# Three loads in place of two for the first block of x, and five pieces in place of six for w2, in a fused attention and gated-FFN kernel

## Chip, cores and metric

One core of one Trainium2 chip. The experiments ran on five different chips, each next to the kernel before in the same rounds. The metric is the device time of one execution in microseconds (us). The span of a trace is 1.8 us shorter than the time of the same execution: 1936.4 against 1938.2 in the profiled run of the kernel before. A "look" below is one profiled run; a load "lands" when the profile shows all of it arrived.

## The reference, cut to what matters

```python
x = A_x                                   # 1 x 2048 x 640, bf16
xn = layernorm(x)
# attention, 32 heads of 192, 2048 keys:
q = (xn @ wq) per head;  p = softmax(q k^T * 192**-0.5);  s = (p v) @ wo
# gated FFN on the same xn:
g = silu((silu(xn @ w1) * (xn @ w3)) @ w2)
return x + s * g
```

## The kernel before

The stream of work is 32 heads x 4 blocks of 512 queries, and TensorE (PE) is busy in it almost without a gap. What matters here is the head of the kernel, in which block 0 of x is loaded, normalised and transposed before PE has anything useful to do.

```python
def load_x(g, t0=0, t1=4, queue=nc.sync):        # row tiles t0..t1 of block g
    queue.dma_start(out=x_sb[:, 4 * g + t0:4 * g + t1, :],
                    in_=x2[g * 512:(g + 1) * 512, :].rearrange("(p t) d -> p t d", t=4)[:, t0:t1, :])

def swap_halves(g):                              # SBUF to SBUF, behind the transposes
    qs = slice(g * 512, (g + 1) * 512)
    nc.sync.dma_start(out=xnS[0:64, :, qs], in_=xnT[64:P, :, qs])
    nc.sync.dma_start(out=xnS[64:P, :, qs], in_=xnT[0:64, :, qs])

def head_start():
    load_x(0, 0, 2)                # SP queue
    load_x(0, 2, 4)                # SP queue
    load_k0(0, nc.sync)            # half of K of head 0
    load_w0()                      # weights of head 0, three loads on the GpSimd queue
    turn_over(44)                  # 44 matmuls without a use, to keep PE going
    ln_stats(0, 0)                 # VectorE, row tile 0
    ln_stats(0, 1)                 # VectorE, row tile 1
    ln_stats_act(0, 3)             # ScalarE, row tile 3: two passes with sums
    load_k0(1, nc.scalar)          # these three loads stand behind tile 3 on ScalarE
    load_x(1, queue=nc.scalar)
    load_v(0, (0,), nc.scalar)
    ln_stats(0, 2)                 # VectorE, row tile 2
    ...                            # rstd of tiles 2 and 3: needs ScalarE's sum
    for i in range(4):
        ln_norm(0, i, nc.vector)
    ln_turn(0, 0, nc.scalar.copy)  # PE: the first transposes ("pst")
    turn_k0(pk0, 0, range(4))      # PE: transposes of K ("pk")
    ...
    swap_halves(0)
    ...
    project_first()                # q of head 0, then the first scores ("st")

# in the stream, at head 16:
for c0, c1 in _pieces(FC, -(-FC // 6)):          # six pieces of two chunks
    nc.sync.dma_start(out=wrest["w2"][:, c0:c1, :], in_=B_w2...[:, c0:c1, :])
```

`x2...rearrange("(p t) d")` gives each partition four consecutive rows. A load of two tiles has 128 contiguous pieces of 2,560 bytes, a load of one tile 128 of 1,280 bytes.

## Time and profile before

| | before |
|---|---|
| time, median of 3 runs | 1938.26 us (1937.99 to 1938.29) |
| PE busy | 1926.6 of 1936.4 us |
| tile 0's statistics start on VectorE | 3.58 us |
| ScalarE's first pass over tile 3 starts | 4.66 us |
| PE's first transposes start | 7.60 us |
| first score matmul | 13.10 us |
| first matmul that reads the swapped half xnS | 19.05 us |

The page's lines, the chain of waits in the head and the pause at 19.05 us are shown in the prediction. Lines of the timeline: columns are start, length, engine, line, operation, output<-input, count, and in brackets the idle time ahead with what ended it.

```profile
2.77 3.89 PE L572 MATMUL pk<-ident_bf 128*128 128x128 bf16 x44 [2.77 <-POOL ident_bf masks.py:199]
...
8.25 1.06 PE L271 MATMUL pk<-ident_bf,kn 128*128 128x128 bf16 x16
```

The 44 filler matmuls end at 6.66 and the first transposes start at 7.60, so PE pauses 0.94 us. The 16 transposes of K take 1.06 us.

### The profile page before, as it was taken

What the parts mean: (1) busy time and instruction counts of PE and PEld (TensorE: products, weight loads), DVE (VectorE), ACT (ScalarE), POOL (GpSimd) and SP (SyncE); (2) the same over time, 40 slices, a digit from 0 to 9 for tenths busy, and PEclk for the clock granted to TensorE, in tenths of its full rate; (3) what the DMA queues carried; (4) which work ended last, traced back from release to release, by engine and by line L of the source; (5) the groups of instructions that cost most, each with busy time, mean ns of one, the idle gap of its engine ahead of it and who ended that gap; (6) DMA issues with size and microseconds to landing.
All of it is one profiled execution on the core that took longest, in us unless ns stands there. A gap on an engine that the chain in (4) does not pass through costs nothing.

```text
span 1936.4 us, 59669 instructions
## 1 busy us (share of the span) xinstructions
PE 1926.6 (99%) x27273; PEld 1315.6 (68%) x27281; DVE 654.6 (34%) x997; ACT 1180.0 (61%) x1279; POOL 282.5 (15%) x501
## 2 busy tenths in 40 slices
PE   9999999999999999999999999999999999999998
PEld 6666666666666666666666666666666666577776
DVE  7333333333333333333333333333333334521111
ACT  6677676767676767776777777677767677210000
POOL 3111111111111111111111111111111110000000
PEclk9999999999999999999999999999999999999999
DMA  8643433323333434363434343434334220937783
GB/s 181 129 101 67 98 68 86 84 62 88 59 90 61 100 63 97 68 162 69 101 66 100 69 101 69 101 64 101 69 69 96 58 68 2 260 69 137 151 152 62
DMA packets 394643, 178.98 MB, mean 92 GB/s; under 512 B 341616, under 2 KB 382832, under 8 KB 394384
## 3 DMA queue, kind: packets, MB, share of 16 engines
q1 hardware_dynamic: 371136, 125.32, 31.6%
q0 software_dynamic: 19472, 45.71, 10.0%
q8 instruction: 215, 3.52, 0.8%
q10 hardware_dynamic: 3776, 4.06, 0.7%
q14 instruction: 44, 0.36, 0.1%
HBM read 52.82 MB, written 27.79 MB: 42 GB/s over the span
## 4 chain that ended last, share of the span: by engine, by line
PE 99%; DVE 1%; DMA 0%; ACT 0%; issue 0%; DVEq 0%; ACTq 0%
PE obank L519 35%; PE st L487 34%; PE ps L424 14%; PE ps_s L111 11%; PE ps_f L731 3%; PE ps_gu L705 1%; PE st L488 1%; PE ps L410 0%; DVE stats L316 0%; DMA x_all<-in_A_x_dram 0%; PE ps L391 0%; PE pst L354 0%; PE pk L271 0%; DVE xn L346 0%; ACT pT L493 0%
## 5 line engine op out<-in xcount | busy, mean ns | idle before, releaser
L493 ACT ACTIVATE pT<-st 128x1024 bf16<-128x1024 f32 (+1 forms) x1025 | 1046.1, 1021 | 250.2 <-PE st L488 234.0
L519 PEld LDWEIGHTS <-pT 64*128 64x128 bf16 x16384 | 711.3, 94 | 242.3 <-ACT pT L493 0.6
L519 PE MATMUL obank<-vt,pT 64*128 64x193 bf16 x16384 | 849.7, 243 | 0.0
L487 PE MATMUL st<-qC,KW 64*128 64x512 bf16 x2046 | 605.6, 376 | 0.1
L528 DVE COPY osum<-obank 128x772 f32<-128x772 f32 x128 | 123.1, 962 | 787.1 <-PE obank L519 787.1
L488 PE MATMUL st<-qB,KW 64*128 64x512 bf16 x1024 | 385.0, 376 | 0.0
L487 PE MATMUL st<-qA,KW 64*128 64x512 bf16 x1022 | 384.3, 376 | 0.1
L488 PE MATMUL st<-qC,KW 64*128 64x512 bf16 x1022 | 384.3, 376 | 0.0
L488 PE MATMUL st<-qA,KW 64*128 64x512 bf16 x1022 | 384.3, 376 | 0.0
L487 PEld LDWEIGHTS <-KW 64*128 64x128 bf16 x3068 | 278.5, 94 | 153.7 <-issue 2.1
L424 PE MATMUL ps<-xnT,W 64*128 64x512 bf16 x1280 | 297.2, 376 | 0.0
L424 PE MATMUL ps<-xnS,W 64*128 64x512 bf16 x1280 | 296.0, 376 | 0.0
L488 PEld LDWEIGHTS <-KW 64*128 64x128 bf16 x3068 | 278.5, 94 | 0.5
L377 POOL DMA_DIRECT2D qC<-qA x124 | 65.4, 528 | 1283.0 <-DVE rl_all L535 1268.2
L430 ACT CAST qB<-ps 128x512 bf16<-128x512 f32 x131 | 76.7, 585 | 228.2 <-PE ps L424 222.6
L111 PE MATMUL ps_s<-wo_sb,oT 128*128 128x384 bf16 (+3 forms) x1535 | 208.8, 299 | 0.1
L424 PEld LDWEIGHTS <-W 64*128 64x128 bf16 x2560 | 122.9, 94 | 121.4 <-issue 0.2
L111 PEld LDWEIGHTS <-oT 128*128 128x128 bf16 x1536 | 148.4, 98 | 60.4
L529 DVE TENSOR_TENSOR osum<-osum,obank 128x772 f32<-128x772 f32 x128 | 122.7, 959 | 13.4
L536 DVE TENSOR_TENSOR ostage<-osum,rl_all 128x768 bf16<-128x768 f32 x128 | 122.7, 958 | 6.3 <-DMA o_scr<-ostage 1.9
L465 DVE SCALAR_TENSOR_TENSOR hT<-pt,qB 64x512 bf16<-64x512 bf16 x64 | 43.8, 684 | 197.4 <-ACT pt L464 197.4
L429 DVE CAST qA<-ps 128x512 bf16<-128x512 f32 x131 | 90.6, 692 | 25.3 <-PE ps L410 7.2
(84 smaller groups left out, 621.9 us busy)
## 6 DMA issues: line engine op xcount, KB each, us to landing
o_scr<-ostage SPq DMA_DIRECT2D x16, 1536.0 KB, 10.6
vt<-in_A_v_cache_dram SPq DMA_DIRECT2D x63, 384.0 KB, 5.9
qC<-qA POOLq DMA_DIRECT2D x248, 64.0 KB, 1.9
qC<-qB POOLq DMA_DIRECT2D x124, 64.0 KB, 2.3
wo_sb<-in_A_wo_dram POOLq DMA_DIRECT2D x1, 7680.0 KB, 36.1
W<-in_A_wq_dram POOLq DMA_DIRECT2D x32, 160.0 KB, 3.6
W<-in_B_w_dram POOLq DMA_DIRECT2D x32, 80.0 KB, 3.3
W<-in_A_wq_dram POOLq DMA_DIRECT2D x32, 80.0 KB, 3.0
```

Source lines behind the costliest of these rows:

```text
L111: nc.tensor.matmul(ps[:, 0:w], lhsT=oT[:, k, :], rhs=wo_sb[:, k, c0:c1], start=(k == 0), stop=(k == OC - 1))
L377: nc.gpsimd.dma_start(out=qC[0:64, half, :], in_=qAB[half][64:P, :])
L424: nc.tensor.matmul(ps[:, r * 512:(r + 1) * 512], lhsT=W[rows, j, :], rhs=xs[rows, j // 2, qs], start=(j == 0), stop=(j == 2 * DC - 1))
L429: a = nc.vector.tensor_copy(out=qAB[0][:], in_=ps[:, 0:512])
L430: b = nc.scalar.copy(out=qAB[1][:], in_=ps[:, 512:1024])
L487: nc.tensor.matmul(st2[:, 0:512], lhsT=ka, rhs=qa, start=r == 0 and nr == 3, stop=r == nr - 1)
L488: nc.tensor.matmul(st2[:, 512:1024], lhsT=kb, rhs=qb2, start=r == 0 and nr == 3, stop=r == nr - 1)
L493: nc.scalar.activation(out=pT2[:, c * w:(c + 1) * w], in_=st2[:, c * w:(c + 1) * w], func=ACT.Exp, scale=att_scale)
L519: nc.tensor.matmul(obanks[r][:, j * 256:j * 256 + DH + 1], lhsT=pT2[r * 64:(r + 1) * 64, t * 512 + j * P:t * 512 + (j + 1) * P], rhs=vt[r ...
L528: nc.vector.tensor_copy(out=osum[:], in_=ov[0])
L529: nc.vector.tensor_tensor(out=osum[:], in0=osum[:], in1=ov[1], op=ALU.add)
L536: nc.vector.tensor_tensor(out=ostage[:, qb * 4:qb * 4 + 4, hg * DH:(hg + 1) * DH], in0=osum[:, :, 0:DH], in1=rl.unsqueeze(2).to_broadcast( ...
```

## The change

Its intent: tile 0's statistics can start when 160 KB have landed and not 320, so the chain that begins the kernel gets shorter; and w2 costs the SP queue one issue less.

```diff
-            for c0, c1 in _pieces(FC, -(-FC // 6)):
+            w2_cuts = [FC * i // 5 for i in range(6)]
+            for c0, c1 in zip(w2_cuts, w2_cuts[1:]):
                 nc.sync.dma_start(out=wrest["w2"][:, c0:c1, :], in_=B_w2.rearrange("(c p) d -> p c d", p=P)[:, c0:c1, :])
@@
     def head_start():
 
-        load_x(0, 0, 2)
+        load_x(0, 0, 1)
+        load_x(0, 1, 2)
         load_x(0, 2, 4)
         load_k0(0, nc.sync)
```

## The prediction

> **What bounds the kernel now.** I read the page first (busy shares, the chain that ended last), then that chain in order of time, then busy time by stretch, then the waits around the head, and last the DMA queues in steps of half a microsecond or one.
>
> The page says that TensorE is the bound, and the busy time by stretch says where it is not:
>
> ```profile
> span 1936.4 us, 59669 instructions
> PE 1926.6 (99%) x27273; PEld 1315.6 (68%) x27281; DVE 654.6 (34%) x997; ACT 1180.0 (61%) x1279; POOL 282.5 (15%) x501
> ...
> 0.00:12.50 12.50, 8.79 (x112) 8.32 (x113) 7.10 (x22) 6.39 (x9) 7.23 (x14) 1.00 0.84 245
> ...
> 50.00:831.00 781.00, 780.95 (x12061) 532.07 (x12058) 265.97 (x372) 551.83 (x585) 131.27 (x234) 1.00 0.39 82
> 831.00:882.00 51.00, 51.00 (x794) 34.77 (x790) 17.35 (x24) 36.74 (x41) 8.42 (x15) 1.00 0.57 154
> ```
>
> In a stretch line come its length, then the busy time of PE, PEld, DVE, ACT, POOL, the clock, the DMA share and GB/s. All idle time of PE together is 1936.4 - 1926.6 = 9.8 us. Of it 3.7 us lie in the first 12.5 us, and from 50 to 831 us there is 0.05 us. Most of the rest (5.8 us) lies after 1722 us, in the output, which the change does not touch. So only the head can give anything, and the last stretch shown, in which w2 is loaded, has nothing to give.
>
> The chain in the head, start and length in us:
>
> ```profile
> 0.75 2.81 DMA x_all<-in_A_x_dram
> 3.56 0.02 issue
> 3.58 0.90 DVE stats L316 x2
> ...
> 7.13 0.06 DVE ve L590
> 7.19 0.36 DVE xn L346
> 7.55 0.05 issue
> 7.60 0.81 PE pst L354 x10
> 8.41 0.89 PE pk L271 x16
> ...
> 10.31 2.20 PE ps L391 x20
> ```
>
> The first load of x (two row tiles, 320 KB) lands at 3.56; from there VectorE runs without a pause (statistics of rows 0, 1, 2, then the normalisation at 7.19), and PE's first useful work starts at 7.60. So the chain does begin with the load that the change cuts. But there is a second gate further on. The timeline at 19 us, and below it the DMA issues from 12.1 to 12.4 us (count, KB each, us to landing):
>
> ```profile
> 18.76 0.10 PEld L424 LDWEIGHTS <-W 64*128 64x128 bf16 x2
> 18.84 0.38 PE L424 MATMUL ps<-xnT,W 64*128 64x512 bf16 x1
> 19.05 0.39 PE L424 MATMUL ps<-xnS,W 64*128 64x512 bf16 x2
> 19.05 1.82 PEld L424 LDWEIGHTS <-W 64*128 64x128 bf16 x18 [0.19 <-issue]
> ...
> xnS<-xnT SPq DMA_DIRECT2D x1, 320.0 KB, 7.4
> ```
>
> Everywhere later (46.39, for one) the xnT and the xnS matmul of a pair start together, and the chain gives the 20 matmuls 2.16 us; here the xnS one starts 0.21 us late and the 20 take 2.36 us in the chain. The last line is the copy of one half of the normalised x to the other 64 partitions (the half swap, two transfers), issued on SP at 11.57 and landing 7.4 us later, at 18.97: just before 19.05. The profile calls the pause "issue", but I read it as a wait for that transfer. So PE already waits some 0.2 us for a DMA at 19.05, and whatever is won before it counts only if that DMA lands earlier too.
>
> Does it? The queues by stretch (q1 is SP's, q10 ACT's, q0 GpSimd's), for 9 to 10, 12 to 13 and 14 to 15 us:
>
> ```profile
> q10 hardware_dynamic: 184, 0.35, 99.9%
> ...
> q0 software_dynamic: 82, 0.14, 92.6%
> ...
> q1 hardware_dynamic: 192, 0.19, 106.3%
> ```
>
> Each line is packets, MB, share of the 16 engines. From about 6.6 to 11.4 us the engines serve what ACT issued at 5.53 to 6.44 (half of K, x of block 1, half of V); then to about 13 the weights of head 1, which GpSimd had issued from 8.05 on; only then the half swap, issued at 10.81. It is a backlog, worked off at a share of about 1.
>
> **What the Trainium skill says.** "Perfetto Trace Analysis", DMA Optimizations: splitting a DMA lets some pieces start sooner, and it adds the condition that the DMA engines are generally idle. Before 2 us the trace agrees; from 2.5 us on the share is 0.87 to 1, so the condition doesn't hold behind the first tile. "DMA: Bandwidth & Descriptors", Issuing engines are not separate DMA queues: transfers of all issuers run on the same 16 engines, and the issuing engine only saves issue time. The trace agrees: one queue's transfers wait while another's are served. The same page, Why small descriptors are slow, gives each packet a fixed overhead; the trace has it too, larger, as worked out below.
>
> **The change part by part.**
>
> *First tile of x alone.* 160 KB instead of 320 KB. SP's queue moved 0.12 MB from 1.5 to 2.5 us and 0.38 MB in the next microsecond; 0.328 MB are reached at about 3.05, 0.164 MB at about 2.62. The landing came 0.5 us after the first of these, so tile 0 lands at about 3.1 instead of 3.56: -0.45 us for the first statistics.
>
> *Second tile alone.* It lands at about 3.6. VectorE needs it 1.07 us after it began tile 0, at 4.2: hidden.
>
> *Tiles 2 and 3 one issue later.* An issue on SP takes 0.44 us (0.88 for two). Issued at 1.63 instead of 1.19, with a first byte 1.0 us after issue (0.75 to about 1.75 in the trace), the third load can run from 2.65, before the first two are through at 3.05. So the issue itself is hidden. But the cut rows give 256 packets of 1,280 B for 128 of 2,560 B. From 8 to 9 us packets of about 4,240 B took 0.944 x 16 / 92 = 164 ns; from 2.5 to 3.5 us those of about 2,330 B took 16 / 163 = 98 ns; the line through both has 17 ns per packet. 8 more per engine: +0.14 us. So tiles 2 and 3 land at about 4.75 instead of 4.62.
>
> *Chain to PE.* VectorE runs 0.45 us earlier up to the step at L590, which needs ScalarE's sum over tile 3 (ready at 6.45, now about 6.6). It would get there at 7.05 - 0.45 = 6.6: a tie. PE's first transposes then start at about 7.2 instead of 7.6, and its K transposes, which need K landed (1.68 + 6.0 = 7.68), at about 7.8 to 7.9. So PE is some 0.3 to 0.4 us ahead at 13 us.
>
> *At 19.05.* The half swap is issued 0.3 to 0.4 us earlier, but into the same backlog. That backlog starts with ACT's issues, which follow ScalarE's first pass over tile 3 (landing 4.62, pass from 4.66, issue 5.53), and before it, from 6 to 7 us, the DMA engines are partly idle (121 and 189 GB/s). So the whole queue hangs on tile 3, which is not earlier but about 0.14 us later. I therefore choose: the swap lands at 18.97 + 0.0 to 0.15, PE waits 0.6 us there instead of 0.2, and the 0.3 to 0.4 us are given back.
>
> *w2 in five pieces.* Chunks 2, 2, 3, 2, 3 instead of six times 2: one issue of about 0.5 us fewer on SP at 840 us, the same bytes. The loads land by about 858 us, the first reader of that tile starts at 1644, and PE is 51.00 us busy in the 51 us around them. 0.0 us.
>
> *Sum.* Head -0.35, given back at 19.05 +0.35, later landing of tile 3 +0.1, w2 0.0: +0.1 us, 1938.36. I pull that to 1938.2 for the second rival below.
>
> **Rivals.**
> 1. The head's gain goes through to the end: the swap is issued 0.4 us earlier and lands 0.4 us earlier. For it: its packets alone are on the engines from 13 us on, so a latency of the SBUF-to-SBUF copy and not the backlog might set its landing. Against it: first packets appear 1.5 us or more after the issue, exactly when the queues before it end. Time 1937.85.
> 2. Part of it goes through: the swap's packets get in among the weights of head 1. Time about 1938.05.
> 3. ScalarE's tile 3 and with it every transfer behind comes the whole issue time later (0.44 us), if the loads are not pipelined as I assume. The chain from tile 3 then delays the swap by as much. Against it: the loads were served without a gap before. Time 1938.7.
> 4. A result over 2% needs 39 us, four times PE's whole idle time to gain, or a new wait repeated in all 128 blocks to lose; nothing in the change touches a block after the first but w2's loads.
>
> **Range and chances.** The mechanism gives 1937.85 (everything goes through) to 1938.7 (whole issue time lost); the three runs of before spread by 0.3 us. I give half to "given back", a third to rivals 1 and 2, the rest to rival 3: 1938.2, range 1937.7 to 1938.6. Within 2% is all but certain: 0.98, 0.01 each side for what I can't see.
>
> **What would show it.** Tile 0's statistics start at about 3.1 and tile 3's ScalarE pass at about 4.7 to 4.8; PE's first transposes at about 7.2; the first xnS matmul again at 19.0 to 19.2, with a longer pause on PE or in its weight loads before it; blocks from 50 us on as before, shifted by one constant. I am wrong if that matmul starts at 18.7 or earlier (rival 1), if tile 3's pass starts after 5.0 (rival 3), or if the distance from there to the end changes by over 0.2 us.

## The result, and the profile after

| | before, same rounds | after |
|---|---|---|
| time, median of 6 runs | 1938.13 us (1937.98 to 1938.29) | 1940.18 us (1939.72 to 1942.64) |
| ratio after / before | | 1.0013, 95% interval 1.0000 to 1.0026 |

Ratios in this document are the mean time of one kernel's fast runs over that of the other's of the same rounds, so they are not quite the ratio of the medians quoted. The kernel got slower by 2 us, one part in a thousand, where I had predicted 1938.2, within 0.1 us of before, and 1938.6 at most. Its runs also spread over 2.92 us, those of before in the same rounds over 0.31. In later rounds before itself spread over up to 1.6 us (1938.03 to 1939.63), so the spread of these rounds was on the small side.

The page of the changed kernel, then the same two stretches of the stream as in the prediction (length, busy time of PE, PEld, DVE, ACT, POOL, clock, DMA share, GB/s):

```profile
span 1938.4 us, 59669 instructions
...
PE 1928.8 (100%) x27273; PEld 1317.7 (68%) x27281; DVE 654.4 (34%) x997; ACT 1181.3 (61%) x1279; POOL 282.4 (15%) x501
```

```profile
50.00:831.00 781.00, 780.95 (x12055) 531.90 (x12054) 267.80 (x375) 551.66 (x585) 131.48 (x234) 1.00 0.39 82
831.00:882.00 51.00, 51.00 (x798) 34.89 (x794) 16.85 (x24) 36.91 (x41) 8.40 (x15) 1.00 0.58 155
```

The span grew by 2.0 us and PE's busy time by 2.2 us (1928.8 - 1926.6) with the same number of instructions. From 50 us on nothing moved, w2's stretch included: PE is busy 780.95 of 781 us and 51.00 of 51 us as before. PE did not wait longer in total; some of its matmuls ran longer. Both effects must lie in the head. The chain there:

```profile
1.68 4.56 DMA x_all<-in_A_x_dram
6.24 0.02 issue
6.26 0.84 ACT xn L338 x2
...
8.07 0.15 DVE ve L592
8.23 0.36 DVE xn L346
...
8.64 1.25 PE pst L354 x10
9.89 1.71 PE pk L271 x16
...
21.46 2.16 PE ps L424 x20
```

It no longer begins with tile 0 but with the third load, which SP issued at 1.68 us and which landed 4.56 us later. ScalarE's pass over tile 3 starts at 6.26, 1.60 us later than before. The timeline of the same stretch:

```profile
2.77 4.87 PE L573 MATMUL pk<-ident_bf 128*128 128x128 bf16 x44 [2.77 <-POOL ident_bf masks.py:199]
3.04 0.89 DVE L316 BATCH_NORM_STATS2 stats<-x_all 128x6 f32<-128x320 bf16 x2 [1.99 <-DMA x_all<-in_A_x_dram]
...
6.26 0.89 DVE L316 BATCH_NORM_STATS2 stats<-x_all 128x6 f32<-128x320 bf16 x2 [0.89 <-DMA x_all<-in_A_x_dram]
...
9.68 1.91 PE L271 MATMUL pk<-ident_bf,kn 128*128 128x128 bf16 x16
...
21.30 0.38 PE L424 MATMUL ps<-xnT,W 64*128 64x512 bf16 x1
21.31 0.59 PE L424 MATMUL ps<-xnS,W 64*128 64x512 bf16 x2
```

Tile 0's statistics do start 0.54 us earlier (3.04), as intended. But VectorE then waits 0.89 us for the third load at tile 2. And the filler takes 4.87 us where it took 3.89, the transposes of K 1.91 us where they took 1.06: PE runs at half its clock here. At 21.3 the xnT and the xnS matmul start together, so the pause for the half swap, 0.2 us before, is gone.

That gives the account of the two profiled runs, event by event:

| from the start to ... | before | after | added in this step |
|---|---|---|---|
| ScalarE's pass over tile 3 | 4.66 | 6.26 | +1.60 |
| PE's first transposes | 7.60 | 8.64 | -0.56 (VectorE had done rows 0 and 1 earlier) |
| first score matmul | 13.10 | 15.56 | +1.42 (PE at half clock) |
| first matmul on V | 14.74 | 17.20 | 0.00 |
| first xnS matmul | 19.05 | 21.31 | -0.20 (no pause for the swap) |
| second projection (L410) | 24.84 | 26.96 | -0.14 |
| end | 1936.43 | 1938.43 | -0.12 |

The sum is +2.00 us. It stands at +2.12 by the second projection and at the last matmul (end at 1931.23 and 1933.35); the last -0.12 comes behind that, in the output. So two things need an explanation: a late third load, worth 1.04 us at the first transposes, and a lost clock, worth 1.42.

### The clock

The trace has records of the clock that PE was granted. In before the full clock is granted at 5.45 us; in after at 11.82. (Ahead of the first such record the stretch view prints 1.00, which is why I read the head from the lengths of the matmuls.) Successive changes lie 3.413 us or a multiple of it apart (5.77, 9.18 and 12.60 in x_only_again), and their phase differs from one execution to the next. The Trainium skill, "TensorE: Matmul & The Clock Gate", Part 1: The HAM clock gate, says the same: a free-running window of 3413 ns, clock states of 4/8 and 8/8, and "the default state is throttled, and activity releases the throttle". In after, the window that would have ended at 8.41 holds the end of the filler at 7.64 and an idle PE behind it, and the grant came one window later. In x23_act, whose window ended at 8.35, the transposes began at 8.30 and the grant came. So I put the lost clock down to the late load and the phase together; for this one execution that is argued, not tested.

### The late load

The trace also records each packet. The packets of 2,560 bytes are the two-tile loads. I counted how many started in each 0.2 us (my own count from the trace's DMA records; 36 packets of before started ahead of its first bin):

```
kernel   first bin at   packets started per 0.2 us
before   2.4 us         24 31 30 29 28 30 31 13 3 1      (256 in both loads; last at 4.2)
after    2.8 us         3 7 11 14 19 24 22 7 3 2 2 3 5 5 1   (128; last at 5.6)
```

In before they run evenly to the end. In after most are through by 4.4, and the rest trickle on until 5.75. The records don't name an engine, but for each load there are 16 packets of 4 bytes (64 for the four loads on this queue), which I read as one engine each closing its share: for the third load twelve came between 3.87 and 4.60, the next not before 5.37. So four engines were late. The skill, "DMA: Bandwidth & Descriptors", Why a DMA increments its semaphore by 16 and not by 1, says that a DMA's engines finish independently and that it has landed only when all have. The trace agrees: the pass on tile 3 waits for the four.

### The profile page after: what moved, and what is told of

Its sections match the earlier page's. It is cut to its first block, busy times and chain, and to the rows that moved or that the text cites. A ratio compares the mean times of both kernels' runs of the same rounds, so it can differ in the third digit from the quotient of the medians.

```text
span 1938.4 us, 59669 instructions
## 1 busy us (share of the span) xinstructions
PE 1928.8 (100%) x27273; PEld 1317.7 (68%) x27281; DVE 654.4 (34%) x997; ACT 1181.3 (61%) x1279; POOL 282.4 (15%) x501
## 4 chain that ended last, share of the span: by engine, by line
PE 99%; DVE 0%; DMA 0%; ACT 0%; issue 0%; SPq 0%; ACTq 0%; DVEq 0%
PE obank L519 35%; PE st L487 34%; PE ps L424 14%; PE ps_s L111 11%; PE ps_f L733 3%; PE ps_gu L707 1%; PE st L488 1%; PE ps L410 0%; DMA x_all<-in_A_x_dram 0%; PE pst L354 0%; PE ps L391 0%; PE pk L271 0%; DVE xn L346 0%; ACT pT L493 0%; DVE osum L529 0%
```

## The experiments

Theories, A to C from the start, D and E as the others weakened. A: the w2 split has nothing to do with it, the x split all. B: the weights of head 0, issued by GpSimd at 1.30 us, get in ahead of the third load because it now comes later (my first theory). C: packets of 1,280 bytes are slow. D: a load that is issued on the SP queue at 1.68 us instead of 1.2 us lands late whatever stands before it. E (the "dry queue" of the expectations): the small loads ahead leave the queue empty before the third load's packets come. The mark in each run is the start of ScalarE's pass over tile 3: 4.66 us in before, 6.26 in after.

All timings are medians, with the lowest and highest run. Before's median was 1938.35 in the rounds of the first four kernels, 1938.35 in those of the next four, then 1938.17, 1938.76 and 1938.05.

### x_only: the x split alone

```diff
 (changed kernel)
-            w2_cuts = [FC * i // 5 for i in range(6)]
-            for c0, c1 in zip(w2_cuts, w2_cuts[1:]):
+            for c0, c1 in _pieces(FC, -(-FC // 6)):
```

> The split of x alone, w2 still in six pieces. My theory (the whole loss is in the head: tiles 2 and 3 of x land late, GpSimd's weight load having come on some DMA engines first): as the changed kernel, 1939.7 to 1942, tile 3's ScalarE pass starts after 6.0 us. Rival (w2's pieces or the count of transfers matter): within 0.3 us of the kernel before, 1938.1.

Measured: 1938.98 us (1938.54 to 1940.21), ratio 1.0002 (0.9986 to 1.0019). Tile 3's pass at 6.72 in the profiled run, which was the 1940.21. PE kept its clock in it (transposes to scores 5.49 us, as in before) and lost 0.37 us to V, which ScalarE issues behind tile 3 and which now held up the first matmul on it. The two runs at 1938.54 show that the split is not always so dear; I have no trace of them. The median lies below the 1939.7 that I had expected at the least; only the mark came as expected.

### w2_only: the w2 pieces alone

```diff
 (changed kernel)
-        load_x(0, 0, 1)
-        load_x(0, 1, 2)
+        load_x(0, 0, 2)
```

> w2 in five pieces alone, x in two loads as before. My theory: 1938.1, the same as before to 0.3 us, tile 3's pass at 4.7. Rival (w2's pieces carry some of the loss): over 1938.6.

Measured: 1938.19 us (1937.92 to 1938.35), ratio 0.9998; tile 3's pass at 4.71. The w2 pieces cost and give nothing. Theory A holds on this side.

### w0_late: the weights of head 0 issued 1.7 us later

```diff
 (changed kernel)
+        nc.gpsimd.memset(hT[:, 0, :], 0.0)
         load_w0()
```

The memset occupies GpSimd until 2.98, where the first weight load is then issued; hT is written again long before it is read.

> The changed kernel with one memset of 128x2048 on GpSimd ahead of head 0's weight loads, so that they are issued about 1 us or more later. My theory (the weights overtake tiles 2 and 3 on some DMA engines): tile 3's pass starts at 4.7 to 5.1 instead of 6.26, and the time falls to 1937.8 to 1938.6. Rival (the third load is slow by itself, from its later issue or from the smaller packets before it): the pass still starts after 5.8, the time stays over 1939.5.

Measured: 1939.03 us (1938.68 to 1939.53), ratio 1.0003; tile 3's pass at 5.96. With no weight load issued before 2.98 us, and no packet of one before 5.25, it is still 1.3 us late. Theory B, which had said 4.7 to 5.1, is badly hurt; the time lies between what the two sides had said (up to 1938.6, over 1939.5). What the run shows besides is the gate at the half swap, in its timeline:

```profile
19.58 0.38 PE L424 MATMUL ps<-xnT,W 64*128 64x512 bf16 x1
20.44 0.39 PE L424 MATMUL ps<-xnS,W 64*128 64x512 bf16 x2 [0.49 <-DMA xnS<-xnT]
```

The xnS matmul starts 0.86 us after the xnT one, with PE idle for 0.49 of it, and the profile now names the transfer. (Pauses at the swap are counted here from start to start, as the 0.2 us of before.)

### before_gap: the kernel before with a tiny load between the two

```diff
 (kernel before)
         load_x(0, 0, 2)
+        gap = const.tile([P, 16], BF16, name="gap")
+        nc.sync.dma_start(out=gap[:], in_=A_wq[0:P, 0:16])
         load_x(0, 2, 4)
```

The second half of x becomes the third load, issued at 1.68, but no packet of x is smaller than before.

> The kernel before with one tiny extra load (128 rows of 32 B) on SP between the two loads of x, so the second is issued one issue later but x's packets stay 2,560 B. If the later issue is what lets the weights in front: tile 3's pass starts after 5.5 and the time is 1939 to 1941. If the small packets of the cut tiles are the cause: the pass at 4.7 to 5.0, time 1938.0 to 1938.4.

Measured: 1940.72 us (1940.49 to 1942.86), ratio 1.0015. In its timeline:

```profile
6.87 0.74 ACT L338 ACTIVATE xn<-x_all 128x640 bf16<-128x640 bf16 x1 [4.83 <-DMA x_all<-in_A_x_dram]
```

A load of 4 KB, and the loss is all there. Theory C (small packets of x) is not needed; D is what remains. What "late issue" means is the question of the following runs.

### after_again: the changed kernel once more

> The changed kernel itself, in the same rounds as the kernel with the x part alone. If w2's five pieces cost nothing, its runs fall among those of the x part alone (1938.5 to 1942.6) and the two means differ by under 0.6 us; if they cost something, it is over 1 us slower in the same rounds. In the profile, tile 3's ScalarE pass starts after 5.8 us again.

Measured: 1940.53 us (1937.99 to 1941.06), ratio 1.0008. Tile 3's pass at 5.89; this profiled run (1938.97) kept its clock and paused 0.33 us at the swap. One of five runs lay at the time of before. The loss repeats, and its size changes from run to run.

### x_only_again: the x split alone once more

> The x part alone, for comparison with the changed kernel in the same rounds: mean within 0.6 us of it, 1938.5 to 1942; tile 3's pass starts after 5.8 us. The rival (w2 matters) has it at 1938.5 to 1939.2 with the changed kernel a full us slower.

Measured: 1940.65 us (1940.41 to 1941.67), ratio 1.0012; tile 3's pass at 6.60. On this chip it is at least as slow as the whole change in the same rounds: its mean is 1.1 us above, where I had expected a difference under 0.6, and in the direction that w2's pieces can't explain. The x split carries all of it.

### x23_act: the third load on ScalarE's queue

```diff
 (changed kernel)
-        load_x(0, 2, 4)
+        load_x(0, 2, 4, nc.scalar)
```

> The changed kernel with tiles 2 and 3 issued from ScalarE's queue, so they are the first transfer of their queue, and K is the third of SP's instead of the fourth. New theory (the third transfer in a row on one queue is served late on some DMA engines, whatever it carries, the weights not being the cause): tile 3's pass starts at 3.8 to 4.9, the time falls to 1937.7 to 1938.6. Rival (x in more than two loads is slow as such): pass after 5.5, time over 1939.

Measured: 1938.31 us (1938.24 to 1938.51), ratio 0.9998. Its timeline:

```profile
4.28 0.89 DVE L316 BATCH_NORM_STATS2 stats<-x_all 128x6 f32<-128x320 bf16 x2 [3.23 <-DMA x_all<-in_A_x_dram]
4.49 0.74 ACT L338 ACTIVATE xn<-x_all 128x640 bf16<-128x640 bf16 x1 [2.00 <-DMA x_all<-in_A_x_dram]
```

Tile 3 is in time and the loss is gone, spread included. The gain at tile 0 is gone as well: its statistics start at 4.28 and not at 3.04, and packets of both queues' loads are under way together (SP's from 1.77 us on, ScalarE's from 1.97 to 4.1). That the one slows the other is my reading.

### before_wait: the kernel before with its second load held back

```diff
 (kernel before)
         load_x(0, 0, 2)
+        for _ in range(2):
+            nc.vector.memset(x_sb[:, 2:4, :], 0.0)
         load_x(0, 2, 4)
```

The load must wait for VectorE's memsets of its destination and is issued at 2.52, later than the 1.6 to 2.0 that I had expected.

> The kernel before with two memsets on VectorE of the place of tiles 2 and 3, so that their load, still SP's second, is issued later, at about 1.6 to 2.0 us. If the place in the queue matters and not the moment: tile 3's pass starts no more than 0.5 us after what the later issue accounts for, by 5.2, time 1938.0 to 1938.8. If the moment of issue is what matters (the load then comes into competition with something else): pass after 5.7, time 1939 to 1941.

Measured: 1941.15 us (1940.63 to 1944.12), ratio 1.0017; tile 3's pass at 7.09, so the load landed 4.6 us after its issue, where the second load of before took 3.4. It is not the place as third load: the second one comes late too if it is issued late.

### x23_first: the large load first

```diff
 (changed kernel)
+        load_x(0, 2, 4)
         load_x(0, 0, 1)
         load_x(0, 1, 2)
-        load_x(0, 2, 4)
```

> The changed kernel with the same three loads of x in another order: tiles 2 and 3 (320 KB) first, then tile 0, then tile 1. The third load is again issued at 1.63 to 1.68 us, but 492 KB instead of 328 KB lie before it. If a queue that has run dry is what makes the third load late (in the changed kernel its first packets come when the first two loads are nearly through): no gap, all of x through by 4.5 us, tile 3's pass at 3.6 to 3.9, time 1937.8 to 1938.8. If the third load is late because it is issued at that moment or is the third: tile 1's statistics wait until after 5.0 and the time is over 1939.

Measured: 1941.30 us (1938.31 to 1942.28), ratio 1.0017. The profiled run was the one at 1938.31: tile 3's pass at 3.67, and tile 1, now the third load, in time. The four others were slow, so the profile had caught the exception.

### warm54: ten more filler matmuls

```diff
 (changed kernel)
-        turn_over(44)
+        turn_over(54)
```

> The changed kernel with 54 instead of 44 idle-filling matmuls on PE, so that PE has no pause between them and the first transposes. If the pause of about 1 us, which the late tile makes, is what delays the full PE clock in some executions (a loss of 1.4 to 1.5 us where it happened): runs of 1941 and more vanish, the spread shrinks to under 1.5 us, the mean is 0.4 to 1.2 us under the changed kernel's, 1938.5 to 1940. If the clock has nothing to do with the pause: 1939.7 to 1942.6 as before.

Measured: 1939.83 us (1939.09 to 1940.95), ratio 1.0010 (0.9996 to 1.0023). Tile 3's pass at 5.96, the clock kept. The filler did not close the pause in this look: it ended at 7.64 as in after, because the clock was granted at 6.33, and the pause was 0.70 us. No run over 1941 us, while three of the changed kernel's eleven were; the mean is still 1.8 us above that of before, so the filler doesn't mend the load. The difference from the changed kernel is too small for these intervals, and the spread (1.86 us) is over the 1.5 that I had expected.

### now0: no weights at all while x is loaded

```diff
 (changed kernel)
-        load_w0()
         turn_over(44)
         ln_stats(0, 0)
         ln_stats(0, 1)
+        load_w0()
```

The weights come too late for the projection, so the time means nothing; only the landing of x is of interest.

> The changed kernel with head 0's weight loads moved behind GpSimd's first power, so none of their packets or issues is there before about 6 us. The time says nothing (the weights come too late). If the weights are what holds up tiles 2 and 3: tile 3's pass at 4.6 to 5.0. If the dry queue alone does it: 5.2 to 6.0, with a drop of the rate to under 200 GB/s at 3.0 to 3.6 us.

Measured: 1943.59 us, median of two. Tile 3's pass at 5.29, and 175 GB/s from 3.0 to 3.6 us: both as the dry queue (E) had it. But no engine was far behind: the last packet of the third load ended at 4.95, and it landed 3.59 us after its issue, near the 3.43 of before's second load.

### kn_second: K in the second place, x's second load in the third

```diff
 (kernel before)
         load_x(0, 0, 2)
-        load_x(0, 2, 4)
         load_k0(0, nc.sync)
+        load_x(0, 2, 4)
```

> The kernel before with the first half of K loaded between the two loads of x: tiles 2 and 3 are third and issued at 1.63, but with 713 KB ahead of them their queue can't run dry. Dry queue as the cause: K through by about 4.3 and tiles 2 and 3 straight behind it, the pass at 5.3 to 5.8 because of the bytes ahead alone, no drop of the rate at 3.0 to 3.6 us. Third place or moment as the cause: pass after 6.5.

Measured: 1941.23 us (two runs, 1941.16 and 1941.29), ratio 1.0015; tile 3's pass at 7.08. Here 384 KB of K lie ahead of the third load, so its queue cannot have run dry (K's packets run on until 4.3, its own start at 3.8), and it is late all the same: landed 5.4 us after its issue, while K in second place took 3.4.

### w0_sp: the weights of head 0 on the SP queue, behind K

```diff
 (changed kernel, in load_w0, three times)
-        nc.gpsimd.dma_start(out=W[...], in_=...)
+        nc.sync.dma_start(out=W[...], in_=...)
```

> The changed kernel with head 0's weights loaded from SP's queue, behind the first half of K, instead of from GpSimd's: same bytes, but they can't come in front of tiles 2 and 3. If half of the delay is the weights served beside tiles 2 and 3 and half the later issue with its gap: tile 3's pass at 5.1 to 5.5 instead of 5.9 to 6.7, the time 1938.4 to 1939.4. If the later issue alone does it: pass still 5.9 to 6.7, time 1939.7 to 1941.5.

Measured: 1940.03 us (1939.66 to 1940.21), ratio 1.0006; tile 3's pass at 6.17. With nothing on GpSimd's queue and the weights behind the third load on the same queue, it is as late as ever. No weight packet started before 5.16 here. Theory B as the cause is dead. The run also shows the clock at its plainest, busy time by stretch:

```profile
5.50:8.80 3.30, 0.68 (x13) 0.51 (x10) 2.07 (x7) 1.75 (x4) 1.27 (x2) 1.00 0.82 178
8.90:12.20 3.30, 3.30 (x34) 3.30 (x33) 0.93 (x2) 2.07 (x2) 2.42 (x4) 0.50 0.96 337
12.30:15.60 3.30, 3.17 (x37) 2.76 (x35) 2.35 (x5) 1.82 (x5) 0.00 (x0) 1.00 0.94 165
```

The filler ended at 5.93 and the transposes came at 8.55. PE was busy 0.68 of 3.30 us, and the clock, already granted, fell to 0.50 for the whole next window, the one in which PE had work without a gap.

### x0_x13: tile 0 alone, tiles 1 to 3 together

```diff
 (changed kernel)
         load_x(0, 0, 1)
-        load_x(0, 1, 2)
-        load_x(0, 2, 4)
+        load_x(0, 1, 4)
```

> x of block 0 in two loads, tile 0 alone and then tiles 1 to 3 together (480 KB), so nothing of x is issued after 1.63 us, though the first tile is small. If what hurts is a load of x issued third, at 1.68: tile 0 at 3.0 to 3.1, tiles 1 to 3 at 4.4 to 4.7, time 1937.8 to 1938.5, spread under 1 us. If the small first load is what hurts (its packets, or the queue running dry behind it): pass after 5.2, time over 1939.

Measured: 1938.32 us (1937.99 to 1939.84), ratio 1.0000. Its timeline:

```profile
3.04 0.89 DVE L316 BATCH_NORM_STATS2 stats<-x_all 128x6 f32<-128x320 bf16 x2 [1.98 <-DMA x_all<-in_A_x_dram]
4.78 0.74 ACT L338 ACTIVATE xn<-x_all 128x640 bf16<-128x640 bf16 x1 [2.75 <-DMA x_all<-in_A_x_dram]
```

The small first load and its 1,280-byte packets are here, and tile 0 is as early as in the changed kernel; the rest of x is second, issued at 1.2, and lands 3.5 us later with tile 3 in time. The queue had even thinned out before most of its packets came (9, 5, 7, 9 of them per 0.2 us from 2.4 to 3.2, then 19 to 21). So neither small packets (C) nor a queue that runs low (E) makes a load late by itself. Nothing is gained at the end either: PE's first transposes start at 7.81, because tile 1 now comes only with the last of x. The runs spread over 1.85 us, more than the 1 us expected; before spread over 1.46 in the same rounds.

### now0_again: the look at now0 once more

> A second look at the changed kernel without head 0's weights before 6 us, for the spread: tile 3's pass at 5.1 to 5.5 again if the first look (5.29) was typical; over 5.8 if it was luck and the weights do not matter.

One look, 1942.47 us. Tile 3's pass at 6.27, as in the changed kernel, with no weight load issued before 6.16. Fifteen engines had closed their share between 4.17 and 4.76; the load's last seven packets moved from 5.2 to 5.9, so one engine was late. So without the weights the load can be late or not.

### w0_late_again: the look at w0_late once more

> A second look at the changed kernel with the weights issued 1.7 us later, in the first look at 5.96 for tile 3's pass and 1938.7 to 1939.5 in time. If the weights are half of the cause, the time is again under 1939.6 in every round and the pass at 5.2 to 6.0; if not, the times are 1939.7 to 1942 as the changed kernel's.

Measured: 1939.29 us (1938.98 to 1939.58), ratio 1.0003; tile 3's pass at 6.11, and a pause of 0.66 us at the swap. So 5.96 was no accident. Yet all eight runs of this kernel lie between 1938.68 and 1939.58, below most of the changed kernel's: the time came as expected if the weights are half of the cause, the pass at 6.11 did not. In both its profiles the memset also delays the filler (start at 3.08 instead of 2.77), PE pauses 0.77 and 1.12 us before the transposes, and the clock is kept. That fits the lower times, but two looks don't show it for the other runs.

### all_later: everything in the head of before held back by 1.7 us

```diff
 (kernel before)
     def head_start():
 
+        for _ in range(2):
+            nc.vector.memset(x_sb[:, 0:2, :], 0.0)
         load_x(0, 0, 2)
         load_x(0, 2, 4)
         load_k0(0, nc.sync)
+        nc.gpsimd.memset(hT[:, 0, :], 0.0)
         load_w0()
```

> The kernel before with everything in its head shifted by about 1.7 us: two memsets on VectorE hold the first load of x until about 2.5 us, one on GpSimd holds the weights until about 3.0; order and spacing stay. If the moment (any load issued after about 1.6 us) is what scatters a transfer over the engines: tiles 2 and 3 land 4.2 us or more after their issue, as in before_wait (4.6). If the spacing to the first load is what matters: 3.3 to 3.7 us after their issue, as in the kernel before (3.4), and the time is 1.7 us over it, 1939.6 to 1940.4.

Measured: 1941.60 us (two runs, 1940.38 and 1942.83), of which 1.7 us are the delay itself; the spacing theory had said 1939.6 to 1940.4. The two loads of x are issued at 2.52 and 2.98 and land 3.1 and 3.4 us later (2.8 and 3.4 in before), without stragglers. So it is not the absolute moment of 1.68 us but the distance from the loads ahead. Two memsets of this size on VectorE stood ahead of the late load in before_wait too, so they are not the cause there. What is lost beyond the 1.7 us lies with the clock, which this profiled run was granted only at 15.65.

### x23_first_again: the large load first, once more

> A second look at the order tiles 2 and 3, tile 0, tile 1, whose profiled run took 1938.3 but whose timed runs took 1940.7 to 1942.3. If the third load (tile 1, issued at 1.68) is late in most executions: tile 1's statistics start after 5.4 here, and the time is over 1940. If the x loads are innocent there: tile 1's statistics at 5.1 to 5.3 again, and a time over 1940 has to show elsewhere in the head, in the PE clock or in K.

Measured: 1942.05 us (two runs, 1941.83 and 1942.27), ratio 1.0020. This time the profile has a slow run, and its chain reads:

```profile
1.68 5.54 DMA x_all<-in_A_x_dram
7.24 0.90 DVE stats L316 x2
```

The late one is again the third load, though it is now tile 1 with only 160 KB: 5.54 us. Most of its engines were through by 4.24; its last 13 packets moved on one or two engines, between 4.4 and 6.3.

### What the looks say together

A load of x issued on SP 0.9 us or more after the first one (at 1.68, or at 2.52 in before_wait) was late in 13 of 15 looks: it landed 4.2 to 5.5 us after its issue. The exceptions are the first looks of x23_first (2.9) and of now0 (3.6). A load of x issued on SP within 0.5 us of the first, or on ScalarE's queue at once, was in time in 5 of 5 (before, w2_only, x23_act, x0_x13, all_later; 3.4 to 3.7). In before itself the first half of K is such a late-issued load: issued at 1.68, twelve engines done between 4.83 and 5.64, four between 6.64 and 6.89; nothing waits for it there. In x0_x13, though, the same load of K, issued at 1.68 too, came evenly (4.93 to 5.76).

That the weights add a part is not excluded. Tile 3's pass started at 6.29 on average in the five looks with the change's x loads and the weights in their old place, and at 5.96 in the five with the weights later or on another queue; the two groups overlap.

The border agrees with the moment at which the engines begin to move the first load's packets, about 1.0 us after that load's issue (1.78 in before, 3.56 in all_later). Loads of x whose issue was over by then came through evenly. Of the late ones most had one to four engines up to 2 us behind the others, before_gap had seven, and in before_wait the whole load started late (first packet at 4.0). This is a pattern that fits most runs, not a mechanism that they show, and between 0.5 and 0.9 us nothing was tried. Why it is those engines, and what they do meanwhile, stays open.

For the clock, take the pause of PE between the end of the filler and its first transposes:

| kernel (look) | pause, us | clock | transposes to scores, us |
|---|---|---|---|
| before | 0.94 | kept | 5.50 |
| x_only | 1.47 | kept | 5.49 |
| before_gap | 1.74 | kept | 5.50 |
| kn_second | 2.12 | lost | 7.13 |
| x_only_again | 2.17 | lost | 7.05 |
| w0_sp | 2.62 | lost | 7.08 |
| before_wait | 2.67 | lost | 6.89 |
| x23_first_again | 2.86 | lost | 7.05 |

With the clock granted before or during it, a pause up to 1.74 us cost nothing, and one from 2.12 us on cost 1.4 to 1.6 us more. In after (pause 1.00) and all_later (1.69) the clock was not lost but granted late. The length of the pause need not be what counts: laid out in windows of 3.413 us from the clock's changes, PE was busy 0.55 to 1.30 us in the window that lost the clock in these looks and 1.68 or more where it was kept. Neither border is clean, for in now0 the clock fell again at 12.57, after a window with 1.80 us busy and pauses of only 1.15 and 0.47. The late load sets the pause, and the phase of the window decides what becomes of it. How often each happens can make the wide spread of these kernels; for the runs without a trace it is not shown.

## Why the prediction was wrong

- **Tile 0 at about 3.1: right.** 3.04 (3.02 in the repeat). Tile 1 hidden: right, its statistics followed at 4.09 without a wait.
- **"Tiles 2 and 3 one issue later ... So the issue itself is hidden": this is the step that failed.** I had put the load at 4.75, 0.14 us late for eight more packets per engine. It landed at 6.24 in after, 1.60 us later than in before, and its first packet started at 2.98 and not at the 2.65 that I had reckoned with. In the eight looks that load x exactly like this (after, after_again, x_only, x_only_again, w0_late, w0_late_again, warm54, w0_sp), with the weights loaded in one way or another, tile 3's pass started at 5.89 to 6.72, 1.2 to 2.1 us later than in before. The packet term was not what grew: before_gap has no smaller packet of x and starts at 6.87. Pipelining of issue and transfer is real on average, since most engines were through by 4.6; but a load waits for its slowest engine, and I had reckoned with the average of the 16.
- **Rival 3 had the direction, and the mark that I had named for it ("if tile 3's pass starts after 5.0") was met, but with little over a quarter of the size**: 0.44 us of issue time, against 1.60 in the profiled run. Its mechanism, that the loads are not pipelined, is not what the packets show. The sign about the end was met as well: from the first xnS matmul to the end it took 0.26 us less than in before, where I had named 0.2.
- **Chain to PE, a tie at L590: the reading was right, the input wrong.** The step did wait for ScalarE's sum (0.49 us at 8.07), and VectorE's head start took 0.56 us off the 1.60.
- **At 19.05, the half swap as second gate: confirmed as a gate, not tested as the place where a gain is lost.** With PE at half clock the pause of 0.2 us vanished. The slow stretch (8.64 to 11.82 in after) put off the swap's issue and PE alike, but not the loads queued ahead of the swap, and its second half landed 6.7 us after its issue in place of 7.4; that this is the reason is not tested. With PE at full clock and tile 3 late the pause grew: 0.86 us in w0_late, 1.03 in before_gap, 0.33 in after_again. So the swap does hang on tile 3. Whether an earlier start of PE would be given back there stays open: no look had PE's first transposes before 7.60. In x0_x13 and x23_act, in which tile 3 is in time, they start at 7.81 and 8.30, and the times equal that of before (1938.32 and 1938.31).
- **w2 at 0.0: right**, by w2_only.
- **Missing altogether: PE's clock.** Before reaches its grant at 5.45 and has a pause of 0.94 us, so nothing in its profile showed that another pause, or another phase, would cost 1.4 us more. I had treated the filler as a fixed 44 matmuls of no importance.
- **The range** was drawn from mechanisms that only shift the head by tenths of a microsecond and from before's spread of 0.3 us. The changed kernel's own runs spread over 2.9 us. The range ended at 1938.6, short of the 1938.7 of rival 3, to which I had given a sixth.
- **Small slips without consequence.** PE's idle time after 1722 us is 5.2 us and not 5.8 (the stretch asked for ran past the end of the span). The DMA share behind 2.5 us is below 0.87 at times (0.76 from 4.0 to 4.5). K was reckoned from an issue at 1.68, but the extra load moves it to 2.15; it landed at 7.78, still before it was needed.

## What to carry to other kernels

Cutting a load so that its first part lands sooner pushes every later load on that queue back by one issue, and the load that matters is the last one that the chain needs. Before cutting, ask which load that is; here it was the third, and cutting without adding a load (tile 0, then all the rest) left it in time. Ask also how long TensorE stands idle before its first real work: here a pause there of 2.12 us or more cost another 1.4 to 1.6 us through the clock.

## What the Trainium skill lacked or had wrong

- "Perfetto Trace Analysis", DMA Optimizations, advises splitting where the engines are idle. It lacks that a load issued some 0.9 us or more after the first, when engines have begun to move packets, can land late because some of its 16 engines come up to 2 us behind the others: 13 of 15 looks here, and 2 us at the end.
- "DMA: Bandwidth & Descriptors", Issuing engines are not separate DMA queues, says that another issuing engine saves issue time only. Here more hung on it: the third load on ScalarE's queue, issued at once, put tile 3's pass at 4.49 in place of 5.89 to 6.72, and the time at 1938.31 in place of 1940.2 to 1940.5. The page lacks that half a microsecond of issue time saved can be worth several times its length.
- "TensorE: Matmul & The Clock Gate", HAM oscillation, warns of idle gaps over about 3.4 us. Here pauses of 2.12 to 2.86 us already cost the clock, and first pauses of up to 1.74 did not; in now0 two of 1.15 and 0.47 in one window did.
- The same page, Part 1, has a busy window of about 3.4 us release the clock. It lacks how busy: in after PE had filled 2.65 of the 3.41 us of the window that ended at 8.41 and got nothing, in before 2.68 of the one that ended at 5.45 and in w2_only 2.65, and got the full clock. In all_later 2.60 got nothing. So the border is at about 2.65 us in these looks, if busy time is what counts.
